# An attention and token-mixing kernel on one Trainium2 core: the second layer of the first group in float32, weight blocks merged in another order, and copies of the prologue moved ahead of exponentials

## The chip, the cores and the metric

The kernel runs on one core of one Trainium2 chip. The metric is the device time of one execution in microseconds (us), as the median of several runs. The engines are named as in the profile: PE (TensorE, its matmuls), PEld (its weight loads), DVE (VectorE), ACT (ScalarE), POOL (GpSimd) and SP (SyncE, which issues the DMAs).

## The reference

Attention with exponential features over 8 batches, 8 heads, 576 rows and 64 columns, followed by a mixing over rows and a two-layer network over the 512 channels:

```python
def phi(x):                                   # w_phi is 64 x 128
    proj = np.einsum('bhsd,df->bhsf', x, w_phi)
    proj = proj - np.max(np.abs(proj), axis=-1, keepdims=True)
    return np.concatenate([np.exp(proj), np.exp(-proj)], axis=-1)
q_p, k_p = phi(q), phi(k)
kv = np.einsum('bhsf,bhsd->bhfd', k_p, v)
num = np.einsum('bhsf,bhfd->bhsd', q_p, kv)
den = np.einsum('bhsf,bhf->bhs', q_p, k_p.sum(axis=2))[..., None] + 1e-06
x = (num / den).transpose(0, 2, 1, 3).reshape(8, 576, 512)
u = x + (x.transpose(0, 2, 1) @ U @ V).transpose(0, 2, 1)    # U 576 x 32, V 32 x 576
out = u + np.maximum(u @ w_ch1, 0.0) @ w_ch2                 # 512 x 2048, 2048 x 512
```

q, k, v and w_phi are float32. U, V, w_ch1 and w_ch2 are float64; the kernel reads them as pairs of 32-bit words and makes float32 of them on the chip.

## The kernel before, in words

**Rows and groups.** The 8 × 576 rows are split into 512 rows of each batch and 64 left over. One batch's 512 rows are a group of the two-layer network; the 64 left over of all eight batches are a ninth group. A group has 16 `hidden` steps (line 688: 128 of the 2048 hidden channels by 512 rows, PSUM tile `ph`) and 16 `add` steps (line 712: those 128 channels times their rows of w2 into four PSUM tiles `o` of 128 rows each). Steps are called chunks; the list `todo` holds them, hidden f ahead of add f − 1.

**Two numbers for one.** The large matmuls run in fp32r. To keep float32's precision each operand is parted: `hi` is the value rounded to fp32r by a copy of ACT, `lo` is what is left, a subtraction on DVE, and a product is made of three matmuls, hi·hi, hi·lo and lo·hi. So a hidden step has 12 matmuls (line 695), an add 12 (line 719). `relu` (line 703) makes h_hi from `ph` on ACT (line 706) and h_lo on DVE (line 707).

**Weight blocks.** w1 and w2 are 32 blocks of 128×512, w1 and w2 in turn. `load_block` (lines 222 and 226) has SP load one of 512 KB into one of four buffers, tag `wide`. `convert` (line 135) takes a float64 apart: on DVE an and (141), a shift with an and (147) and an or (150), on ACT a copy of the low half (144) and a pass with a bias (145). `join` (154, a custom DVE instruction) adds the parts, tile `w_r`; `end_block` makes `w_hi` on ACT (243) and `w_lo` on DVE (244). `conv` does one slot: begin the next block, then end the block before it. The blocks' tiles live in the tags `wh1_f`, `wh2_f` and `wl0` to `wl32`, `w_r` of block i in the place of `wl(i+1)`; some of these places hold early tiles of the prologue before (`home`, line 267). U and V go through the same `convert` and `join`, in `uv_parts` (171 to 207), a generator that does one piece at each `next(uv)`.

**Attention.** A `Pair` is two heads of one batch; there are four to a batch. Its steps are `transpose_both` (T), `copy_both` (ACT copies of T, line 373, DVE's parts of T and tail_T, line 331), `whole_q` and `whole_k` (projections; k features at lines 412 and 414, copies of q at 436), the exponentials (ACT, 421 to 423), `end_q` (DVE's subtraction, 442 and 444, and q's exponentials, after POOL's all-reduce at 437), `s_kv` and `s_out`. Batches from the third on use parted T and w_phi (`w_hl`, `tail_T`; line 451 is the projection of a parted tail). `Tokens` is the mixing over rows with U and V (`split`, `down`, `up`), `Mixer` the two-layer network of one group. `keep_busy` (768) gives PE matmuls to do in waits.

**The order.** The program has two parts. `early` (802) is written by hand: the attention of batch 0, and beside it U, V and the first weight blocks; then, from chunk to chunk of group 0, the attention of pairs 4 to 7 and the other blocks, 23 chunks (hidden 0 to 11 and add 0 to 10) in all. In it PE, ACT, DVE and POOL all keep the order in which the code issues. `chunk(n, blocks)` does n chunks and `blocks` slots of `conv` behind each; a hidden's `relu` is held back until the next chunk (`held`). `ordered` (928) goes to the end of the program; only PE keeps the written order there, and a scheduler places the instructions of the others, into free places of the first part too. `boundary` (905) is the change from one group to the next.

## Time and profile before

| | |
|---|---|
| median of 3 runs | 1221.85 us (1221.19 to 1223.09) |
| the profiled execution, its own time | 1222.26 us |
| its span | 1220.3 us |
| its mean granted clock of TensorE | 0.964 |
| PE busy | 1134.9 us (93%), 9292 instructions |
| DVE busy | 669.6 us (55%), 1371 instructions |
| ACT busy | 537.4 us (44%), 1134 instructions |
| POOL busy | 153.3 us (13%), 119 instructions |
| share of PE's work by line | hidden (695) 235.8 + 229.8 + 229.1 us, add (719) 230.8 + 225.0 + 224.6 us |
| chain that ended last | PE 80%, DVE 11%, ACT 5%, SP's queue 2% |

The span runs from the first to the last instruction of the profiled execution; its time has some 2 us more around it. Busy shares are means over stages of quite different kinds, so the profile has to be read by windows of time. A timeline row has the start, the length, the engine, the line, the operation, out<-in, the tile's size and the number of instructions merged into the row (x1, x2); the bracket is the idle time of the engine just before it and what ended that. A row of the waits is the waiter, the releaser, the total of the waits, their number and the longest one. A matmul of plain float32 leaves two records.

### The profile page before, as it was taken

How to read it: one execution, taken by the hardware profiler on the slowest of the kernel's cores; microseconds unless marked ns; L12 is line 12 of the kernel's file. 1: busy time of each engine (PE TensorE's matmuls, PEld its weight loads, DVE VectorE, ACT ScalarE, POOL GpSimd, SP SyncE). 2: the span in 40 equal slices, each digit the busy share in tenths (PEclk: the TensorE clock that was granted, in tenths of full speed). 3: DMA queues.
4: the chain of work that ended last, by engine and by line, in shares of the span. 5: the costliest groups of instructions: out<-in, count | busy, mean ns of one | idle time of the engine just before them, and what ended most of it. 6: DMA issues, size and time to landing. Idle time of an engine off the chain costs nothing.

```text
span 1220.3 us, 22461 instructions
## 1 busy us (share of the span) xinstructions
PE 1134.9 (93%) x9292; PEld 948.3 (78%) x9300; DVE 669.6 (55%) x1371; ACT 537.4 (44%) x1134; POOL 153.3 (13%) x119
## 2 busy tenths in 40 slices
PE   7756787599999999999999999999999999999997
PEld 5545565488888888888888888888888888888886
DVE  4776777766546655655565556655555644212111
ACT  7566666653445444544544454445443542111010
POOL 3310101110112011201111111111110210000000
PEclk9767988899999999999999999999999999999999
DMA  4344333212111311221113111211122002200001
GB/s 134 94 131 137 116 113 107 75 56 92 40 31 48 110 31 31 57 102 30 39 51 109 31 31 56 86 57 30 30 88 70 21 18 70 91 1 18 18 1 35
DMA packets 90533, 75.74 MB, mean 62 GB/s; under 512 B 51648, under 2 KB 76736, under 8 KB 90304
## 3 DMA queue, kind: packets, MB, share of 16 engines
q1 hardware_dynamic: 90432, 74.31, 20.1%
q8 instruction: 74, 1.21, 0.4%
q14 instruction: 27, 0.22, 0.1%
HBM read 55.41 MB, written 18.87 MB: 61 GB/s over the span
## 4 chain that ended last, share of the span: by engine, by line
PE 80%; DVE 11%; ACT 5%; SPq 2%; issue 1%; DMA 1%; ACTq 0%; DVEq 0%
PE ph L695 30%; PE o L719 29%; PE xp L564 5%; PE kv_ps L539 4%; PE pk L499 2%; PE T L389 2%; PE pp L650 1%; PE pt L682 1%; ACT w_hi L243 1%; DVE w_r L154 1%; DVE w_lo L244 1%; DVE w_r L150 1%; PE pq L520 1%; PE xp L557 1%; PE kv_ps L529 1%
## 5 line engine op out<-in xcount | busy, mean ns | idle before, releaser
L695 PE MATMUL ph<-uT_hi,w_hi 128*128 128x512 f32 x576 | 235.8, 409 | 36.8 <-DVE h_lo L707 33.9
L707 DVE SCALAR_TENSOR_TENSOR h_lo<-ph,h_hi 128x512 fp32r<-128x512 f32 x144 | 99.3, 690 | 282.6 <-ACT h_hi L706 282.6
L706 ACT ACTIVATE h_hi<-ph 128x512 fp32r<-128x512 f32 x144 | 85.8, 596 | 333.2 <-PE ph L695 332.5
L719 PE MATMUL o<-w_hi,h_hi 128*128 128x512 f32 x576 | 230.8, 401 | 0.0
L695 PE MATMUL ph<-uT_lo,w_hi 128*128 128x512 f32 x576 | 229.8, 399 | 0.7 <-DVE uT_lo L262 0.7
L695 PE MATMUL ph<-uT_hi,w_lo 128*128 128x512 f32 x576 | 229.1, 398 | 0.0
L719 PE MATMUL o<-w_hi,h_lo 128*128 128x512 f32 x576 | 225.0, 391 | 0.0
L719 PE MATMUL o<-w_lo,h_hi 128*128 128x512 f32 x576 | 224.6, 390 | 0.0
L695 PEld LDWEIGHTS ph<-uT_hi,w_hi 128*128 128x128 f32 x576 | 111.1, 193 | 63.4 <-DVE h_lo L707 37.2
L437 POOL PARTITION_ALL_REDUCE qp<-qp x64 | 128.1, 2013 | 213.0 <-ACT qp L436 212.4
L695 PEld LDWEIGHTS ph<-uT_hi,w_lo 128*128 128x128 f32 x576 | 110.9, 192 | 24.6
L695 PEld LDWEIGHTS ph<-uT_lo,w_hi 128*128 128x128 f32 x576 | 111.3, 193 | 22.1 <-DVE uT_lo L262 1.3
L719 PEld LDWEIGHTS o<-w_hi,h_lo 128*128 128x128 f32 x576 | 108.1, 188 | 23.4
L719 PEld LDWEIGHTS o<-w_hi,h_hi 128*128 128x128 f32 x576 | 108.3, 188 | 20.5
L719 PEld LDWEIGHTS o<-w_lo,h_hi 128*128 128x128 f32 x576 | 108.5, 188 | 19.9
L437 POOL PARTITION_ALL_REDUCE qp_t<-qp_t x32 | 24.3, 759 | 636.0 <-ACT qp_t L436 636.0
L331 DVE TENSOR_TENSOR T<-T,T 64x512 fp32r<-64x512 f32 x96 | 66.1, 689 | 23.7 <-ACT T L330 21.7
L330 ACT CAST T<-T 64x512 fp32r<-64x512 f32 x96 | 55.8, 581 | 29.2 <-DVE T L331 19.1
L564 PE MATMUL xp<-kv,qp 128*64 128x65 f32 x2048 | 68.5, 227 | 0.0
L564 PEld LDWEIGHTS xp<-kv,qp 128*64 128x64 f32 x2048 | 65.8, 144 | 0.0
L539 PE MATMUL kv_ps<-vb,kp 128*64 128x65 f32 x2048 | 65.4, 221 | 0.2 <-ACT kp L423 0.2
L539 PEld LDWEIGHTS kv_ps<-vb,kp 128*64 128x64 f32 x2048 | 64.3, 138 | 0.3 <-ACT kp L423 0.3
(132 smaller groups left out, 1443.8 us busy)
## 6 DMA issues: line engine op xcount, KB each, us to landing
w<-in_moe_w_ch_dram SPq DMA_DIRECT2D x32, 512.0 KB, 3.7
raw<-in_k_dram SPq DMA_DIRECT2D x32, 256.0 KB, 3.0
raw<-in_q_dram SPq DMA_DIRECT2D x32, 256.0 KB, 2.7
vb<-in_v_dram SPq DMA_DIRECT2D x64, 128.0 KB, 3.1
u_dram<-x SPq DMA_DIRECT2D x32, 256.0 KB, 2.6
st<-u_dram SPq DMA_DIRECT2D x16, 512.0 KB, 3.8
out_dram<-st SPq DMA_DIRECT2D x32, 256.0 KB, 2.8
t_r<-in_k_dram SPq DMA_DIRECT2D x32, 32.0 KB, 2.1
```

Source lines behind the costliest of these rows:

```text
L150: nc.vector.scalar_tensor_tensor(out=a, in0=hi_w, scalar=-0x80000000, in1=a, op0=ALU.bitwise_and, op1=ALU.bitwise_or)
L330: nc.scalar.copy(out=dst[0:D], in_=src)
L331: nc.vector.tensor_sub(dst[D:2 * D], src, f32(dst[0:D]))
L389: nc.tensor.transpose(out=pT[:, c * P:(c + 1) * P], in_=self.raw[n][:, c // 2, c % 2, :], identity=ident)
L437: nc.gpsimd.partition_all_reduce(qp[0], qp[1], P, ReduceOp.absmax)
L499: nc.tensor.matmul(pk[:, i, :, :], self.T[0][:, i, cs], w_hl, start=True, stop=True)
L539: nc.tensor.matmul(self.kv_v[z * HP:(z + 1) * HP, f, g, :], kp[f][:, i, z * HP:(z + 1) * HP], self.vb[:, g, t, :], start=False, stop=(t == ...
L564: nc.tensor.matmul(xv[zs, c, :], qp[f][:, c * P + z * HP:c * P + (z + 1) * HP], self.kv[:, f, c // 2, :], start=(f == 0), stop=(f == 1), s ...
L695: nc.tensor.matmul(ph, l[:, c * P:(c + 1) * P], r[:, c, :], start=(n == 0), stop=(n == len(terms) * NCC - 1))
L706: nc.scalar.activation(out=h_hi, in_=ph, func=AF.Relu)
L707: nc.vector.scalar_tensor_tensor(out=h_lo, in0=ph, scalar=0.0, in1=f32(h_hi), op0=ALU.max, op1=ALU.subtract)
L719: nc.tensor.matmul(self.o[t], l[:, cs], r, start=(f == 0 and n == 0), stop=(f == NFC - 1 and n == len(terms) - 1))
```

## The change

**The second layer of group 0.** `relu` of group 0 writes one float32 tile `h` on ACT and no h_lo. Its `add` multiplies `h` with the merged block `w_r` of w2 (kept in `w_t`) in one float32 matmul a tile in place of three fp32r ones: 4 matmuls a step in place of 12. The parting of w2 moves to `split_w2`, which `hidden` of group 1 calls, one block a step.

**The blocks.** `conv` now begins with ACT's copy of the new block's low half, then merges the block before it (`join`, and w_hi where it is of w1) through the argument `between` of `convert`, then issues the rest of the new block, and then `w_lo` of the block before, where it is of w1. The places of `w_r` change to suit. `chunk` issues its slots of `conv` between a hidden's matmuls and its `relu`; `held` is gone, and the number of slots per chunk is another.

**The prologue and the order.** `copy_both` and `whole_q` of the next pair come ahead of `end_q` of this one; pieces of U and V are converted behind `s_out`; in the last pairs of the first part `end_q` is later.

```diff
-    def convert(st, a, b_):
+    def convert(st, a, b_, between=None):
...
+        nc.scalar.activation(out=bh[:, :, 0], in_=halves[:, :, 1], func=AF.Copy, scale=2.0 ** -13)
+        if between is not None:
+            between()
         nc.vector.tensor_scalar(
             out=bh[:, :, 1], in0=halves[:, :, 3], scalar1=0x7FF0, scalar2=None,
             op0=ALU.bitwise_and)
-        nc.scalar.activation(out=bh[:, :, 0], in_=halves[:, :, 1], func=AF.Copy, scale=2.0 ** -13)
...
+    def merge_block():
+        f, m, b_, r = begun[ended[0]]
+        join(r.bitcast(I32), b_)
+        if m == 2:
+            w_t[f] = r
+            return
+        hi = const.tile([P, C], F32R, tag=f"wh1_{f}", name=f"w_hi1_{f}")
+        nc.scalar.copy(out=hi, in_=r)
+        w_hi_t[1, f] = hi
...
     def end_block():
+        f, m, b_, r = begun[ended[0]]
+        if m == 1:
+            lo = const.tile([P, C], F32R, tag=f"wl{f}", name=f"w_lo1_{f}")
+            nc.vector.tensor_sub(lo, r, f32(w_hi_t[1, f]))
+            w_lo_t[1, f] = lo
...
+    def split_w2(f):
+        r = w_t.pop(f)
+        hi = const.tile([P, C], F32R, tag=f"wh2_{f}", name=f"w_hi2_{f}")
+        lo = const.tile([P, C], F32R, tag=f"wl{NFC + f}", name=f"w_lo2_{f}")
         nc.scalar.copy(out=hi, in_=r)
         nc.vector.tensor_sub(lo, r, f32(hi))
...
     def conv(n=1):
...
+            some = ended[0] < len(begun)
             if len(begun) < NB:
-                begin_block()
-            if ended[0] < len(begun) - 1 or len(begun) == NB and ended[0] < NB:
+                i = len(begun)
+                f, m = i // 2, i % 2 + 1
+                at = NFC + (f + 1 if m == 2 else (f + 2) % (NFC + 1))
...
+                convert(loaded[i], r.bitcast(I32), b_, merge_block if some else None)
+                begun.append((f, m, b_, r))
+            elif some:
+                merge_block()
+            if some:
                 end_block()
...
         def hidden(self, f, later=False):
+            if self.g == 1:
+                split_w2(f)
...
         def relu(self, f, ph):
+            if self.g == 0:
+                h = moe.tile([P, 512], F32, tag="h_hi", bufs=2, name=f"h{self.g}_{f}")
+                nc.scalar.activation(out=h, in_=ph, func=AF.Relu)
+                self.h[f] = h
+                return
...
             terms = self.h[f]
+            if self.g == 0:
+                terms = ((terms, w_t[f]),)
...
     def chunk(n=1, blocks=0):
         for _ in range(n):
             fn, f, *ts = todo.pop(0)
...
+            if fn.__name__ == "hidden":
+                rest = fn(f, True)
+                conv(blocks)
                 rest()
...
             p[i + 1].transpose_both()
             keep_busy(2)
+            p[i + 1].copy_both()
+            p[i + 1].whole_q()
+            keep_busy(2)
             p[i].end_q()
-            p[i + 1].copy_both()
...
             if i == 1:
+                next(uv)
                 next(uv)
                 tk.split(0)
             if i == 2:
+                next(uv)
                 next(uv, None)
-                conv()
+                conv(2)
...
             p[i].whole_k()
+            if i > 5:
+                p[i - 1].end_q()
             chunk(2, 1)
...
+            chunk(2, 1)
             p[i].whole_q()
             chunk(1, 2)
             if i == 6:
                 tk.down(0)
-            p[i].end_q()
-            chunk(1, 1)
-            if i == 7:
-                p[8].transpose_k()
-            chunk(1, 1)
+            if i < 7:
+                chunk(1, 2)
+        p[8].transpose_k()
+        p[7].end_q()
+        chunk(1, 2)
```

Where the instructions stand follows from this and from the scheduler. The first place is a weight block on DVE in the middle of the first part. Before, with w_b and w_r of the block under way, w_r_5 and w_lo_5 of the one before it:

```order
L147 TENSOR_SCALAR w_r_6_1611<-w_6_1416 128x512
L150 SCALAR_TENSOR_TENSOR w_r_6_1611<-w_6_1416,w_r_6_1611 128x512
L154 ISA w_r_5_1566<-w_r_5_1566,w_b_5_1565 128x1024
L244 TENSOR_TENSOR w_lo_5_1619<-w_r_5_1566,w_hi_5_1618 128x512
L141 TENSOR_SCALAR w_b_6_1624<-w_6_1446 128x512
```

The same place on DVE in the changed kernel, with the two blocks numbered 6:

```order
L156 ISA w_r_6_1575<-w_r_6_1575,w_b_6_1574 128x1024
L144 TENSOR_SCALAR w_b_6_1584<-w_6_1514 128x512
L149 TENSOR_SCALAR w_r_6_1585<-w_6_1514 128x512
L152 SCALAR_TENSOR_TENSOR w_r_6_1585<-w_6_1514,w_r_6_1585 128x512
L246 TENSOR_TENSOR w_lo_6_1594<-w_r_6_1575,w_hi_6_1588 128x512
L156 ISA w_r_6_1585<-w_r_6_1585,w_b_6_1584 128x1024
L144 TENSOR_SCALAR w_b_7_1604<-w_7_1530 128x512
```

Between the join (ISA) and the w_lo of a block stand three instructions of the next block, where there was none, and a block of w2 has no w_lo here. The same blocks on ACT, before:

```order
L144 ACTIVATE w_b_6_1610<-w_6_1416 128x512
L145 ACTIVATE w_b_6_1610<-w_b_6_1610,warm 128x512
L243 CAST w_hi_5_1618<-w_r_5_1566 128x512
L144 ACTIVATE w_b_6_1624<-w_6_1446 128x512
L145 ACTIVATE w_b_6_1624<-w_b_6_1624,warm 128x512
L243 CAST w_hi_6_1632<-w_r_6_1611 128x512
```

And in the changed kernel, where h_4 is a float32 tile of group 0 and w_hi_6_3173 the first of the two parts of a w2 block:

```order
L141 ACTIVATE w_b_6_1584<-w_6_1514 128x512
L239 CAST w_hi_6_1588<-w_r_6_1575 128x512
L147 ACTIVATE w_b_6_1584<-w_b_6_1584,warm 128x512
L728 ACTIVATE h_4_1596<-ph_4_1559 128x512
L141 ACTIVATE w_b_7_1604<-w_7_1530 128x512
L255 CAST w_hi_6_3173<-w_r_6_1585 128x512
L147 ACTIVATE w_b_7_1604<-w_b_7_1604,warm 128x512
```

The copy w_hi stands between the two passes of the next block, where it stood behind both; the copies w_hi of w2 (line 255) are issued by group 1 and placed by the scheduler here, a block apart, in the first part.

The second place is DVE at the end of the first part, where tail_T of the first parted pair (line 331 before, 351 after) is made. Before:

```order
L154 ISA w_r_14_2427<-w_r_14_2427,w_b_14_2426 128x1024
L244 TENSOR_TENSOR w_lo_14_2469<-w_r_14_2427,w_hi_14_2468 128x512
L331 TENSOR_TENSOR T_2_0_2480<-T_2_0_2475,T_2_0_2480 64x512 x2
L331 TENSOR_TENSOR tail_T_0_2474<-tT_0_2472,tail_T_0_2474 64x2x64 x2
L707 SCALAR_TENSOR_TENSOR h_lo_11_2502<-ph_11_2447,h_hi_11_2501 128x512
L141 TENSOR_SCALAR w_b_15_2505<-w_15_2412 128x512
L147 TENSOR_SCALAR w_r_15_2506<-w_15_2412 128x512
```

After:

```order
L246 TENSOR_TENSOR w_lo_15_2314<-w_r_15_2297,w_hi_15_2308 128x512
L256 TENSOR_TENSOR w_lo_0_2723<-w_r_0_883,w_hi_0_2722 128x512
L351 TENSOR_TENSOR T_2_0_2326<-T_2_0_2321,T_2_0_2326 64x512
L256 TENSOR_TENSOR w_lo_1_2783<-w_r_1_1112,w_hi_1_2782 128x512
L256 TENSOR_TENSOR w_lo_2_2836<-w_r_2_1195,w_hi_2_2835 128x512
L351 TENSOR_TENSOR T_2_0_2326<-T_2_0_2321,T_2_0_2326 64x512
L351 TENSOR_TENSOR tail_T_0_2320<-tT_0_2318,tail_T_0_2320 64x2x64
L256 TENSOR_TENSOR w_lo_3_2969<-w_r_3_1327,w_hi_3_2968 128x512
L351 TENSOR_TENSOR tail_T_0_2320<-tT_0_2318,tail_T_0_2320 64x2x64
L464 TENSOR_TENSOR qp_3_t<-qp_3_t 128x128
L464 TENSOR_TENSOR qp_3_0_2274<-qp_3_0_2274 128x512
L464 TENSOR_TENSOR qp_3_1_2277<-qp_3_1_2277 128x512
```

Four subtractions of w2's parting (line 256) stand among those of T and tail_T, the q subtractions (line 464) of the last early pair come behind them, and the last block's work, which followed tail_T, is ahead of it.

The third place is ACT in the prologue, at the second pair's q features. Before:

```order
L423 ACTIVATE qp_1_t<-qp_1_t 128x128
L422 ACTIVATE qp_1_00_333<-qp_1_01_334 128x512
L423 ACTIVATE qp_1_01_334<-qp_1_01_334 128x512
L422 ACTIVATE qp_1_10_337<-qp_1_11_338 128x512
L423 ACTIVATE qp_1_11_338<-qp_1_11_338 128x512
L373 COPY T_0_2_436<-T_0_2_438 128x512
L376 COPY tail_T_2_434<-tT_2_448 64x2x64 x2
L379 COPY T_0_2_435<-T_0_2_443 128x512
L144 ACTIVATE u_st<-u_st 128x160
L145 ACTIVATE u_st<-u_st,warm 128x160
L436 COPY qp_2_01_538<-pq_0_2_531 128x512
```

After:

```order
L393 COPY T_0_2_437<-T_0_2_439 128x512
L396 COPY tail_T_2_435<-tT_2_449 64x2x64 x2
L399 COPY T_0_2_436<-T_0_2_444 128x512
L456 COPY qp_2_01_465<-pq_0_2_458 128x512
L456 COPY qp_2_11_469<-pq_0_2_459 128x512
L456 COPY qp_2_t<-pqt_2_462 128x128
L442 ACTIVATE qp_1_t<-qp_1_t 128x128
L443 ACTIVATE qp_1_t<-qp_1_t 128x128
L442 ACTIVATE qp_1_00_278<-qp_1_01_279 128x512
L443 ACTIVATE qp_1_01_279<-qp_1_01_279 128x512
```

The three T copies and three q copies of the third pair now stand ahead of the six q exponentials of the second, and the conversion of U is no longer between them.

More of the change, by code (lines that the diff above doesn't have):

```diff
@@ L207, in uv_parts @@
             nc.vector.tensor_sub(vm[lo], v_f[lo], f32(vm[lo]))
-    w_hi_t, w_lo_t = {}, {}
+    w_hi_t, w_lo_t, w_t = {}, {}, {}
     NB = 2 * NFC
@@ L227, in load_block @@
         loaded.append(st)
-    def begin_block():
-        i = len(begun)
-        f, m = i // 2, i % 2 + 1
-        b_ = const.tile([P, C], I32, tag=f"wh{m}_{f}", name=f"w_b{m}_{f}")
-        r = const.tile([P, C], F32, tag=f"wl{i + 1}", name=f"w_r{m}_{f}")
-        convert(loaded[i], r.bitcast(I32), b_)
-        begun.append((f, m, b_, r))
-    def end_block():
-        i = ended[0]
-        f, m, b_, r = begun[i]
-        join(r.bitcast(I32), b_)
-        hi = const.tile([P, C], F32R, tag=f"wh{m}_{f}", name=f"w_hi{m}_{f}")
-        lo = const.tile([P, C], F32R, tag=f"wl{i}", name=f"w_lo{m}_{f}")
+    def merge_block():
[7 more added lines that the diff above has]
+        w_hi_t[1, f] = hi
+    def end_block():
+        f, m, b_, r = begun[ended[0]]
[3 more added lines that the diff above has]
+            w_lo_t[1, f] = lo
+        begun[ended[0]] = None
+        ended[0] += 1
+    def split_w2(f):
+        r = w_t.pop(f)
+        hi = const.tile([P, C], F32R, tag=f"wh2_{f}", name=f"w_hi2_{f}")
+        lo = const.tile([P, C], F32R, tag=f"wl{NFC + f}", name=f"w_lo2_{f}")
         nc.scalar.copy(out=hi, in_=r)
         nc.vector.tensor_sub(lo, r, f32(hi))
-        w_hi_t[m, f], w_lo_t[m, f] = hi, lo
-        begun[i] = None
-        ended[0] += 1
+        w_hi_t[2, f], w_lo_t[2, f] = hi, lo
     def conv(n=1):
@@ L253, in conv @@
                 load_block()
+            some = ended[0] < len(begun)
             if len(begun) < NB:
-                begin_block()
-            if ended[0] < len(begun) - 1 or len(begun) == NB and ended[0] < NB:
+                i = len(begun)
+                f, m = i // 2, i % 2 + 1
+                at = NFC + (f + 1 if m == 2 else (f + 2) % (NFC + 1))
+                b_ = const.tile([P, C], I32, tag=f"wh{m}_{f}", name=f"w_b{m}_{f}")
+                r = const.tile([P, C], F32, tag=f"wl{at}", name=f"w_r{m}_{f}")
+                convert(loaded[i], r.bitcast(I32), b_, merge_block if some else None)
[3 more added lines that the diff above has]
+            if some:
                 end_block()
@@ L268, in tile_kernel @@
     homes = [f"wh{m}_{f}" for f in range(NFC - 1, KEEP - 1, -1) for m in (1, 2)]
-    homes += [f"wl{i}" for i in range(2 * NFC, 2 * KEEP, -1)]
+    homes += [f"wl{f}" for f in range(NFC - 1, KEEP - 1, -1)]
+    homes += [f"wl{NFC + i}" for i in (*range(NFC, KEEP + 1, -1), 0)]
     home_of = {("xs1", t): homes[t] for t in range(NT + 1)}
@@ L782, in tile_kernel @@
     ORDERED = 7
-    held = []
     def chunk(n=1, blocks=0):
@@ L789, in chunk @@
             fn, f, *ts = todo.pop(0)
-            rest = held.pop() if held else None
-            if rest is not None and fn.__name__ == "hidden":
+            if fn.__name__ == "hidden":
+                rest = fn(f, True)
+                conv(blocks)
                 rest()
-                rest = None
-            if fn.__name__ == "hidden":
-                held.append(fn(f, True))
             else:
                 fn(f, *ts)
-                if rest is not None:
-                    rest()
-            conv(blocks)
+                conv(blocks)
     def early(x, xt):
@@ L822, in early @@
             keep_busy(2)
+            p[i + 1].copy_both()
+            p[i + 1].whole_q()
+            keep_busy(2)
             p[i].end_q()
-            p[i + 1].copy_both()
-            if i == 1:
-                next(uv)
             p[i].s_kv()
             p[i + 2].load_v()
-            keep_busy(2)
-            if i == 2:
-                next(uv)
-            p[i + 1].whole_q()
             p[i + 1].whole_k()
+            keep_busy(1)
             if i == 2:
@@ L861, in early @@
         m = Mixer(0, x)
-        m.transposes(0)
-        m.transposes(1)
-        conv()
-        tk.up(NT)
-        m.transposes(2)
-        m.transposes(3)
-        p[4].end_q()
-        conv(2)
+        for t in range(NT):
+            m.transposes(t)
+        conv(1)
         todo.extend(m.chunks())
@@ L872, in early @@
         p[4].s_kv()
+        tk.up(NT)
+        p[4].end_q()
         chunk(1, 1)
@@ L893, in early @@
                 tk.down(0)
-            p[i].end_q()
-            chunk(1, 1)
-            if i == 7:
-                p[8].transpose_k()
-            chunk(1, 1)
+            if i < 7:
[3 more added lines that the diff above has]
+        chunk(1, 2)
         while ended[0] < NB:
             conv()
-        while held:
-            held.pop()()
         return p[7], p[8], x, xt, tk
```

10 lines of the change are left out of this document (5 added, 5 removed).

## Prediction

> **What bounds the kernel now.** I read the page's slices first, for where TensorE is not full. The rows are the busy tenths of each engine in 40 slices of 30.5 us, and the clock that TensorE was granted.
>
> ```profile
> PE   7756787599999999999999999999999999999997
> DVE  4776777766546655655565556655555644212111
> PEclk9767988899999999999999999999999999999999
> ```
>
> From the ninth slice on PE is full and its clock is high; ahead of that nothing is full. Then I split the span where that changes. The first hidden chunk starts near 94 us and the weights begin to be converted near 62 us. The end of the first stage is the instruction on which PE waits for the last time at length:
>
> ```profile
> 244.65 0.48 PE L451 MATMUL pkt<-w_hl,tail_T 128*128 128x128 f32 x1 [10.93 <-DVE tail_T L331]
> ```
>
> I call this time T*: 244.65 us. The windows around it (window, length, then busy time and count of PE, weight loads, DVE, ACT, POOL, then the granted clock, the DMA engines' share and GB/s):
>
> ```profile
> 0.00:62.00 62.00, 46.67 (x652) 35.51 (x661) 37.69 (x101) 38.34 (x86) 21.45 (x32) 0.89 0.43 119
> 62.00:244.65 182.65, 124.62 (x1053) 97.82 (x1048) 136.66 (x271) 116.57 (x207) 20.83 (x15) 0.82 0.36 112
> 244.65:330.00 85.35, 83.92 (x685) 70.97 (x687) 54.44 (x108) 40.42 (x88) 9.20 (x6) 0.97 0.21 63
> 530.00:1220.30 690.30, 680.44 (x5131) 573.97 (x5128) 324.80 (x650) 248.28 (x543) 69.44 (x45) 1.00 0.15 46
> ```
>
> Behind T* PE is busy 98 to 99% of the time, so what comes there can only get longer by PE's own work. Between 62 and T* PE is busy 68%, DVE 75%, ACT 64%: three engines wait for each other. The chain of waits there, in rows of waiter, releaser, total us, times, longest:
>
> ```profile
> PE ph L695 <- DVE h_lo L707: 28.6, 6, 9.1
> DVE w_lo L244 <- ACT w_hi L243: 26.7, 30, 1.8
> ACT w_hi L243 <- DVE w_r L154: 23.5, 23, 2.1
> ACT w_b L145 <- DVE w_b L141: 16.9, 24, 2.9
> DVE h_lo L707 <- ACT h_hi L706: 12.0, 7, 4.1
> PE pkt L451 <- DVE tail_T L331: 10.9, 1, 10.9
> SPq L226 <- DVE w_r L150: 63.8, 14, 10.5
> SPq L222 <- DVE w_r L150: 41.0, 13, 8.1
> ```
>
> PE waits for DVE, DVE waits for ACT, ACT for DVE again: a ping-pong inside every weight block. One block on DVE, of 30 alike in this stage:
>
> ```profile
> 154.26 0.45 DVE L141 TENSOR_SCALAR w_b<-w 128x512 uint16<-128x512 uint16 x1
> 154.61 0.41 DVE L147 TENSOR_SCALAR w_r<-w 128x512 int32<-128x512 int32 x1
> 155.05 0.69 DVE L150 SCALAR_TENSOR_TENSOR w_r<-w,w_r 128x512 int32<-128x512 int32 x1
> 155.66 0.69 DVE L154 CUSTOM_DVE_ANT_0 w_r<-w_r,w_b 128x1024 uint16<-128x1024 uint16 x1
> 157.08 0.69 DVE L244 TENSOR_TENSOR w_lo<-w_r,w_hi 128x512 fp32r<-128x512 f32 x1 [0.74 <-ACT w_hi L243]
> 157.69 0.45 DVE L141 TENSOR_SCALAR w_b<-w 128x512 uint16<-128x512 uint16 x1
> ```
>
> Start to start the five cost 0.35, 0.44, 0.61, 0.68 (1.42 less the wait) and 0.61 us, 2.69 in all. The wait stands because w_hi reads what the join wrote one instruction earlier, and w_lo reads w_hi.
>
> **The change: the stage from 62 us to T\*.** I take DVE as the pacemaker, the busiest of the three and the releaser in PE's longest waits.
>
> *Work that goes from DVE.* Fifteen of the w_lo of w2 leave (15 × 0.61 = 9.2 us), and eleven h_lo of group 0 (same size and form; 0.61 each is an estimate from the w_lo row, 6.7 us). What comes in ahead of T*: block 15's second half starts earlier, and one join and one w_lo of it are now in front (0.35+0.44+0.61+0.68+0.61 = 2.7). The scheduler does not keep the parting of w2 in group 1: four of the new subtractions stand ahead of the last tail_T (4 × 0.61 = 2.4), and ACT's sixteen copies w_hi of w2 stand right behind the joins, where they stood. So ACT is relieved of nothing. Three q subtractions move behind T* (two of 128x512, one of 128x128: about 1.4). Net −9.2 −6.7 +2.7 +2.4 −1.4 = −12.2 us: DVE's work falls from 136.7 to 124.5.
>
> *Waits that go.* DVE idles 182.65 − 136.66 = 46.0 us. Of it 26.7 is w_lo behind w_hi and 12.0 h_lo behind h_hi, 38.7 together; 7.3 has other causes and stays. The join now has the next block's copy, and the and, shift and or, between it and w_lo, and group 0 has no h_lo.
>
> *Waits that come.* The join now runs first in a slot and needs ACT's bias pass of the block before; w_lo stands behind ACT's exponentials where a slot meets them; ACT's w_hi waits for a join that stands behind k features on DVE. Behind a waiting w_lo or join stand, on DVE, the next block's three instructions and now and then the k features and T subtractions, for which PE waits. ACT work in front costs, from its start times here, 0.63, 0.72 and 0.49 us an instruction:
>
> ```profile
> 98.59 0.76 ACT L144 ACTIVATE w_b<-w 128x512 uint16<-128x512 uint16 x1
> 99.22 0.85 ACT L145 ACTIVATE w_b<-w_b,warm 128x512 uint16<-128x512 uint16 x1
> 99.94 0.59 ACT L243 CAST w_hi<-w_r 128x512 fp32r<-128x512 f32 x1
> ```
>
> I went along the new order with these prices and found some 14 us of waits of 1 to 2.7 us, and add 5 for those I can't see: 19. This is the softest term: 5 at least (one short wait in each of three pairs), at most the 38.7 that went. I take the middle because ACT has 116.6 us of work in a stage of about 150, and can't be early everywhere. Stage: 124.5 + 7.3 + 19 = 150.8 us in place of 182.65.
>
> A cross-check by pairs, from one T copy of ACT to the next:
>
> ```profile
> 114.33:156.96 42.63, 32.22 (x272) 25.38 (x271) 31.24 (x61) 27.63 (x48) 5.18 (x4) 0.92 0.40 123
> 156.96:202.30 45.34, 33.82 (x264) 26.54 (x264) 34.27 (x67) 29.37 (x54) 5.36 (x4) 0.81 0.31 100
> 202.30:244.65 42.35, 29.27 (x263) 22.73 (x261) 31.67 (x63) 27.01 (x49) 4.93 (x3) 0.89 0.31 92
> ```
>
> No engine has over 34.3 us of work in a pair. Walked by hand with the new order and the prices above, these take about 31, 36 and 34.5 us, and the 52.3 us ahead of them 40.5: 142 together. The walk knows only undisturbed instructions, and some are stretched:
>
> ```profile
> 182.24 1.43 DVE L141 TENSOR_SCALAR w_b<-w 128x512 uint16<-128x512 uint16 x1
> ```
>
> That one took 1.43 in place of 0.45. I allow 5.5 us for such over the stage (an estimate, some six of them), 147.5 in all, 3 us from the sum by idle time.
>
> *Ahead of 62 us.* The T and q copies of the next pair now stand ahead of this pair's q exponentials on ACT, and the converting of U and V behind the second and third s_out. Two waits of DVE, the brackets below, are what that is placed on:
>
> ```profile
> 30.21 0.33 DVE L154 CUSTOM_DVE_ANT_0 u_st<-u_st 128x320 uint16<-128x320 uint16 x1 [3.38 <-ACT u_st L145]
> 51.29 0.42 DVE L154 CUSTOM_DVE_ANT_0 v_st<-v_st 128x512 uint16<-128x512 uint16 x1 [3.05 <-ACT v_st L145]
> ```
>
> They are 6.4 us; I take 5.5 (2, if the exponentials that now come later are missed by PE; 8, with the earlier T copies on top). T* falls to 62 − 5.5 + 150.8 = 207.3, that is −37.3 us.
>
> **The change: PE's own work.** Group 0's second layer goes from three f32r matmuls a tile to one in float32. The f32r price, and float32 elsewhere:
>
> ```profile
> 1140.10 0.39 PE L695 MATMUL ph<-uT_hi,w_hi 128*128 128x512 f32 x1
> 1140.32 0.39 PE L695 MATMUL ph<-uT_lo,w_hi 128*128 128x512 f32 x1
> 292.15 2.72 PE o L719 x12
> L480 PE MATMUL pq<-T,w_f x32: 589/664/1217, 6.4 to 222.6; 64*128 64x512 f32 x32
> 17.14 1.13 PE L480 MATMUL pq<-T,w_f 64*128 64x512 f32 x4 [1.41 <-ACT T L373]
> 117.44 0.38 PE L458 MATMUL pkt<-w_f,tail_T 128*128 128x128 f32 x2
> 117.75 1.16 PE L463 MATMUL pk<-w_f,T 64*128 64x128 f32 x16
> ```
>
> An f32r matmul starts every 0.2275 us (2.73 for an add of twelve, 2.72 in the chain) and its record is 0.39 long, so 0.16 of a record is not throughput. The shortest float32 record of the same width is 0.589: less 0.16 that is 0.43, about two passes, and a float32 matmul leaves two records (x2 for one pkt). So 2 × 0.43 = 0.85 to 4 × 0.2275 = 0.91; four make an add of 3.41 to 3.64, and I take 3.55, +0.8. The low end is the four records of pq in 1.13 us as two matmuls one after another, 0.57 each, an add of 2.3 (but these have 64 rows each, and pk's sixteen records in 1.16 us say that such ones run side by side). The high end is the pkt's 0.31 for 128 columns times four: 1.24, an add of 4.96.
>
> The Trainium skill, page FP8 and Floating Point Precision, section TensorE Precision Notes, speaks against the change: float32 takes four passes through the array, one more than the three terms here. An estimate by that rule is 4/3 of 2.73, 3.64, an add dearer by 0.91, where the records give 0.8; no run so far shows the new matmul itself.
>
> Eleven of the sixteen adds come ahead of T*, in PE's 58 us of idle time; five come behind and are paid: +4.0 (−2.1 to +11.2). Behind T* the boundary also gets the moved q subtractions and twelve more w_lo of w2 on DVE. PE is 98% busy there and DVE 64% (54.4 of 85.4 us), so I put +1.0 on it (0 to 2.5). Group 1 on is otherwise the same work under a full PE.
>
> **The sum.** The profiled execution took 1222.26 us for a span of 1220.3, 2.0 us around it, and is 0.4 above the median of the runs shown. 1222.26 − 37.3 + 4.0 + 1.0 = 1190.0 us.
>
> **The rivals.**
>
> *Weak gain.* New waits of DVE on ACT take the place of the old ones in proportion: DVE stays 75% busy, and 124.5 us of work take 124.5/0.748 = 166.4. T* is then 222.9, the time 1205.5. For it: ACT keeps all its work, and the subtractions of w2 land just ahead of T*. Against: the 26.7 us have one cause, a distance of one instruction, and that distance grows. Chance 0.16.
>
> *Dear float32.* An add costs 4.96: five behind T* cost +11.2, and eleven ahead of it 24.5 us more PE work, of which perhaps 5 lands on T* beside the waits. 1222.26 − 37.3 + 5 + 11.2 + 1 = 1202. For it: pkt's spacing. Against: the 0.589 record. Chance 0.08.
>
> *Strong gain.* New waits are only the 5 us: the stage is 136.8, T* 193.3, the time 1176. PE's work up to there (124.6 us now, at a clock of 0.82) would have to fit with the eleven dearer adds. Chance 0.12.
>
> *Slower: the weight blocks' loads set the pace.*
>
> ```profile
> w<-in_moe_w_ch_dram SPq DMA_DIRECT2D x32, 512.0 KB, 3.7
> ```
>
> If one block in four buffers can't be had faster than 182.65/32 = 5.7 us, the stage keeps its length, and only the dearer adds and the boundary are paid: 1222.26 + 5 = 1227. For it: SP stands 104.8 us in these loads. Against: what SP waits for is DVE's w_r that frees the buffer, a load lands in 3.7 us with others under way, and no engine's wait on a load is among the rows above. Chance 0.04.
>
> *The change doesn't do what it says.* In part that is seen already: w_hi of w2 stays early. Were the stage all ACT's, nothing would come of it, 1222. Chance 0.02.
>
> **How the numbers follow.** Forecast 0.58: 1190. The rivals are 0.16 (1205.5), 0.08 (1202), 0.12 (1176), 0.04 (1227), 0.02 (1222). The range takes in the weak gain and the dear float32 up to 1207, and reaches down to 1177, which the forecast gives with new waits of 6 us; what is left out is the strong gain beyond that and the two cases at 1222 and above. About 0.2%, 2.4 us, is what a measurement of this kernel can tell from no change. Faster 0.94, same 0.02, slower 0.04.
>
> **What would show it.** In the profile after: w_lo's waits on w_hi fall from 26.7 to under 10 us and no h_lo of group 0 is there; the last tail_T releases PE near 207 us; an add of group 0 takes 3.4 to 3.7 us in the chain; behind T* PE stays full, with some 980 us to the end. It is wrong if T* stays above 223, if DVE is still idle for over 35 us ahead of it, or if an add takes over 4.5 us.

## The result, and the profile after

The changed kernel takes 1183.72 us (median of 4 runs, 1182.8 to 1187.0); the kernel before, run beside it, 1221.98 us. The ratio is 0.969, with an interval of 0.967 to 0.971: 38 us less, where 32 were forecast. The profiled execution took 1184.01 us, its span is 1182.1 us.

The page's slices of the changed kernel (29.6 us each now):

```profile
PE   8759988999999999999999999999999999999997
DVE  4788898666565556555565656655665535112111
PEclk9869998999999999999999999999999999999999
```

TensorE still has its thin place in the third slice, but from the fourth on it is at 80% or more and the clock stays high; VectorE is at 80% or more from the third slice to the seventh, where before it was at 60 to 80%. The end of the first stage, T*:

```profile
203.69 0.47 PE L471 MATMUL pkt<-w_hl,tail_T 128*128 128x128 f32 x1 [5.39 <-DVE tail_T L351]
```

T* went from 244.65 to 203.7 us, 41 us earlier, and PE's wait for tail_T there is half as long. The windows (columns as before), the first from 62 us to T*, the second from there, and then the first one cut where the first hidden chunk begins:

```profile
62.00:203.70 141.70, 121.79 (x979) 83.41 (x980) 121.32 (x246) 109.06 (x202) 21.36 (x15) 0.91 0.46 143
203.70:330.00 126.30, 125.03 (x1051) 99.78 (x1052) 77.34 (x159) 57.44 (x129) 16.50 (x11) 0.98 0.18 53
62.00:88.15 26.15, 16.70 (x127) 12.88 (x128) 21.10 (x47) 18.94 (x40) 5.20 (x4) 0.63 0.47 153
88.15:203.70 115.55, 105.10 (x852) 70.53 (x852) 100.22 (x200) 90.12 (x163) 16.16 (x11) 0.97 0.46 141
```

VectorE's work in the stage fell from 136.66 to 121.32 us, its idle time from 46.0 to 20.4 (141.70 − 121.32). Of the 41 us, 15 are less work and 26 are less waiting. From the first hidden on, PE is busy 105.1 of 115.6 us. The waits of the stage:

```profile
ACT w_hi L255 <- DVE w_r L156: 10.9, 9, 2.8
DVE w_r L156 <- ACT w_b L147: 7.6, 4, 2.6
PE pkt L478 <- issue: 11.6, 3, 7.6
PE pkt L471 <- DVE tail_T L351: 5.4, 1, 5.4
DVE w_lo L246 <- ACT w_hi L239: 5.4, 4, 2.0
ACT w_hi L239 <- DVE w_r L156: 4.1, 6, 1.2
```

PE's 28.6 us behind h_lo are gone with h_lo itself; w_lo waits for w_hi 4 times and not 30 times. New are the joins that wait for ACT's bias pass (w_r behind w_b, 7.6 us) and TensorE's 7.6 us ahead of a pkt. How the ping-pong went is to be seen in two weight blocks on DVE:

```profile
117.75 0.69 DVE L156 CUSTOM_DVE_ANT_0 w_r<-w_r,w_b 128x1024 uint16<-128x1024 uint16 x1
118.36 0.46 DVE L144 TENSOR_SCALAR w_b<-w 128x512 uint16<-128x512 uint16 x1
...
119.76 0.68 DVE L246 TENSOR_TENSOR w_lo<-w_r,w_hi 128x512 fp32r<-128x512 f32 x1
120.36 0.69 DVE L156 CUSTOM_DVE_ANT_0 w_r<-w_r,w_b 128x1024 uint16<-128x1024 uint16 x1
...
124.56 1.64 DVE L156 CUSTOM_DVE_ANT_0 w_r<-w_r,w_b 128x1024 uint16<-128x1024 uint16 x1 [2.10 <-ACT w_b L147]
```

The join at 117.75 and its w_lo at 119.76 have three instructions between them, and the w_lo has no bracket. The join at 124.56 shows the new wait: ACT does q copies (an attention step) ahead of the bias pass. This join is also stretched, 1.64 us in place of 0.69; what such rows have in common stands in the last section.

```profile
121.89 1.08 ACT L456 COPY qp<-pq 128x512 f32<-128x512 f32 x2 [0.18 <-PE pq L500]
122.85 0.28 ACT L456 COPY qp_t<-pqt 128x128 f32<-128x128 f32 x1
123.01 0.81 ACT L141 ACTIVATE w_b<-w 128x512 uint16<-128x512 uint16 x1
123.66 0.87 ACT L147 ACTIVATE w_b<-w_b,warm 128x512 uint16<-128x512 uint16 x1
```

An add of group 0 in the chain, two of those behind T*, and the record of its float32 matmuls (two to a matmul):

```profile
210.12 3.44 PE o L748 x8
222.04 3.43 PE o L748 x8
L748 PE MATMUL o<-w_r,h x40: 590/592/595, 210.0 to 245.8; 128*128 128x512 f32 x40
```

It takes 3.44 us, with a record every 0.43 us (each is 0.59 long), beside 2.73 before.

### The profile page after: what moved, and what is told of

Its sections match the earlier page's. It is cut to its first block, busy times and chain, and to the rows that moved or that the text cites. A ratio compares the mean times of both kernels' runs of the same rounds, so it can differ in the third digit from the quotient of the medians.

```text
span 1182.1 us, 22322 instructions
## 1 busy us (share of the span) xinstructions
PE 1134.0 (96%) x9231; PEld 928.6 (79%) x9236; DVE 655.9 (55%) x1355; ACT 531.9 (45%) x1134; POOL 153.5 (13%) x119
## 4 chain that ended last, share of the span: by engine, by line
PE 86%; DVE 8%; ACT 3%; issue 2%; DMA 1%; POOL 0%; SPq 0%; DVEq 0%; POOLq 0%; ACTq 0%
PE ph L717 31%; PE o L748 31%; PE kv_ps L559 5%; PE xp L584 4%; PE pk L519 2%; PE pp L670 2%; PE T L409 2%; PE pt L702 1%; PE kv_ps L549 1%; DVE w_r L156 1%; PE pq L540 1%; PE pq L541 1%; PE xp L577 1%; DVE w_r L152 1%; PE vp L686 1%
## 5 line engine op out<-in xcount | busy, mean ns | idle before, releaser
L734 DVE SCALAR_TENSOR_TENSOR h_lo<-ph,h_hi 128x512 fp32r<-128x512 f32 x128 | 88.3, 690 | 265.3 <-ACT h_hi L733 265.3
L717 PE MATMUL ph<-uT_lo,w_hi 128*128 128x512 f32 x576 | 225.9, 392 | 0.2 <-DVE uT_lo L281 0.2
L717 PE MATMUL ph<-uT_hi,w_lo 128*128 128x512 f32 x576 | 225.5, 391 | 0.0
L733 ACT ACTIVATE h_hi<-ph 128x512 fp32r<-128x512 f32 x128 | 76.3, 596 | 326.8 <-PE ph L717 326.3
L748 PE MATMUL o<-w_hi,h_hi 128*128 128x512 f32 x512 | 204.7, 400 | 0.0
L748 PE MATMUL o<-w_hi,h_lo 128*128 128x512 f32 x512 | 199.9, 390 | 0.0
L748 PE MATMUL o<-w_lo,h_hi 128*128 128x512 f32 x512 | 199.6, 390 | 0.0
L748 PEld LDWEIGHTS o<-w_hi,h_lo 128*128 128x128 f32 x512 | 96.1, 188 | 20.9
L748 PEld LDWEIGHTS o<-w_hi,h_hi 128*128 128x128 f32 x512 | 96.3, 188 | 18.2
L748 PEld LDWEIGHTS o<-w_lo,h_hi 128*128 128x128 f32 x512 | 96.4, 188 | 17.8
L350 ACT CAST T<-T 64x512 fp32r<-64x512 f32 x96 | 55.8, 581 | 29.6 <-DVE T L351 19.5
```

Source lines behind the costliest of these rows:

```text
L350: nc.scalar.copy(out=dst[0:D], in_=src)
L717: nc.tensor.matmul(ph, l[:, c * P:(c + 1) * P], r[:, c, :], start=(n == 0), stop=(n == len(terms) * NCC - 1))
L733: nc.scalar.activation(out=h_hi, in_=ph, func=AF.Relu)
L734: nc.vector.scalar_tensor_tensor(out=h_lo, in0=ph, scalar=0.0, in1=f32(h_hi), op0=ALU.max, op1=ALU.subtract)
L748: nc.tensor.matmul(self.o[t], l[:, cs], r, start=(f == 0 and n == 0), stop=(f == NFC - 1 and n == len(terms) - 1))
```

## The experiments

Times are medians; ratios are to the kernel before, run beside each on the same chip. Theory one says that VectorE, with its waits on ScalarE, sets the first stage; theory two has another cause in each run. T* is read in each as above.

### One edit taken back: the second layer in f32r

```diff
-        if m == 2:
-            w_t[f] = r
-            return
+        # w_hi and w_lo of both matrices in merge_block and end_block
-            if self.g == 0:
-                terms = ((terms, w_t[f]),)
```

h_lo of group 0 and the places of the tiles also go back to what they were before.

> The changed kernel, but group 0's second layer stays in three f32r matmuls a tile, with h_lo, and w2 is parted as its blocks are merged; block order and prologue are those of the change. Theory one (VectorE and its waits on ScalarE set the first stage): VectorE gets back fifteen w_lo of w2 and eleven h_lo at 0.61 us, 16 us, and up to 9 us of waits behind h_hi, so the stage ends 16 to 25 us later than at 203.7, at 220 to 229 us; five adds behind it are 0.7 us cheaper each. Time 1196 to 1205 us. Theory two (with the float32 layer or not, TensorE sets the stage once the blocks are in the new order): eleven adds are 0.7 us cheaper each, the stage ends at 204 or earlier, time 1176 to 1181.

Measured: 1189.9 us, ratio 0.974 (0.9725 to 0.9754). T* is 213.2, 9.5 us later than in the changed kernel, and the rest of the program 3 us shorter (975.4 in place of 978.4). Neither number fits: float32 is worth 6 us here, not 12 to 21, and not less than nothing. The window to T* and the waits:

```profile
62.00:213.20 151.20, 118.86 (x1024) 93.52 (x1024) 135.55 (x269) 110.11 (x202) 22.89 (x15) 0.88 0.44 136
```

```profile
DVE w_lo L242 <- ACT w_hi L236: 7.1, 5, 2.0
DVE h_lo L722 <- ACT h_hi L721: 2.1, 4, 0.5
```

VectorE has nearly the work of before, 135.6 us, in 151.2 us: it is 90% busy. So the rest of the change takes most of the waits out without float32, those behind h_hi too (the run with neither edit, below, shows that these don't need the order inside a block either). What float32 takes away on top is 14.2 us of work, of which a third comes back as idle time (15.7 us here, 20.4 with float32).

### Float32 alone

```diff
 (before.py)
+            if self.g == 0:
+                terms = ((terms, w_t[f]),)
+        if m == 2:
+            w_t[f] = r
+            return
```

The edit also moves the parting of w2 to group 1 and places the tiles as the change does; blocks, chunks and prologue are those of before.

> The kernel before with the float32 second layer of group 0 and the later parting of w2 alone; block order, chunks and prologue as before. Theory one: VectorE loses 16 us of work, 12 us of waits behind h_hi and the waits behind w_hi of the sixteen w2 blocks (half of 26.7, 13 us), less new waits; the stage ends 20 to 35 us ahead of 244.65 and the time is 1190 to 1206 us. Theory two (the block order is what frees the stage): the pairs of w_hi and w_lo of w1 still stand next to each other and the gain is under 12 us, 1211 us or more.

Measured: 1197.55 us, ratio 0.980 (0.9785 to 0.9814), inside theory one's range. T* is 217.5.

```profile
62.00:217.50 155.50, 123.53 (x1000) 84.33 (x996) 122.81 (x245) 112.79 (x206) 22.03 (x15) 0.89 0.43 131
```

```profile
DVE w_lo L249 <- ACT w_hi L248: 15.8, 15, 2.1
```

Work fell by 13.9 us and idle time by 13.3 (46.0 to 32.7). The w_lo of w1 still waits, 15 times for 1.05 us.

### A block's pieces in the old order

```diff
-        nc.scalar.activation(out=bh[:, :, 0], ...)
-        if between is not None:
-            between()
         nc.vector.tensor_scalar(out=bh[:, :, 1], ...)
+        nc.scalar.activation(out=bh[:, :, 0], ...)
...
         nc.vector.scalar_tensor_tensor(out=a, ...)
+        if between is not None:
+            between()
```

> The changed kernel, but a block's pieces on VectorE and ScalarE stand as before: and, copy, bias, shift, or, then join, w_hi and w_lo of the block before it next to each other. Theory one: sixteen w_lo of w1 wait again for the w_hi right ahead, 0.9 us each as before (26.7/30), 14 us, of which what stands ahead of the stage's end is paid; time 1192 to 1198 us. Theory two (TensorE sets the stage, 96 to 99% busy between 88 and 160 us): most of it is hidden, 1183 to 1187 us.

Measured: 1192.68 us, ratio 0.977 (0.9751 to 0.9787), as theory one has it. T* is 210.2.

```profile
62.00:210.20 148.20, 120.66 (x979) 81.88 (x979) 121.94 (x245) 110.23 (x202) 21.99 (x15) 0.94 0.44 136
```

```profile
DVE w_lo L246 <- ACT w_hi L239: 20.3, 16, 3.6
```

The work is the same, only waits come: 14.9 us more behind w_hi, and 6.4 less behind the bias pass (1.2 in place of 7.6).

### Neither of the two

The first and the third edit together.

> Neither the float32 second layer nor the new order inside a block: group 0 in f32r with w2 parted at once, join, w_hi and w_lo next to each other as before; what is left of the change is the prologue, the slots per chunk, the relu behind the slots and the later end_q. Theory one (float32 and the order inside a block remove the same waits, so that each alone does most of it): without both the waits of w_lo and h_lo come back and the stage ends at 225 to 240 us, time 1203 to 1217. Theory two (the slots and the place of relu and end_q do it, the other two add 6 and 9 us each on top): 1184 + 6 + 9, 1197 to 1201.

Measured: 1213.43 us, ratio 0.993 (0.9916 to 0.9947), T* 233.6: theory one.

```profile
62.00:233.59 171.59, 124.14 (x1022) 97.41 (x1023) 135.60 (x268) 113.03 (x201) 20.81 (x15) 0.86 0.38 117
```

```profile
DVE w_lo L242 <- ACT w_hi L236: 29.8, 31, 2.7
PE ph L710 <- DVE h_lo L722: 12.6, 5, 6.5
```

With this run the four corners are known, all of them with the rest of the change in place. The times are in us, and the columns on VectorE are for the window from 62 us to T*:

| | median | T* | VectorE's work | its idle time | w_lo behind w_hi | join behind bias pass |
|---|---|---|---|---|---|---|
| neither | 1213.4 | 233.6 | 135.6 | 36.0 | 29.8 | none |
| float32 alone | 1192.7 | 210.2 | 121.9 | 26.3 | 20.3 | 1.2 |
| the block's order alone | 1189.9 | 213.2 | 135.6 | 15.7 | 7.1 | none |
| both | 1183.7 | 203.7 | 121.3 | 20.4 | 5.4 | 7.6 |

Each alone gives 21 and 24 us, the second to come only 6 or 9. The work that float32 takes away is the same in both rows, 14 us; what doesn't add up is the idle time. It falls by 9.7 us with float32 and by 20.3 with the order, but only by 15.6 with both. Some 8 us of the difference are waits of w_lo that either edit removes, and 6 are the joins behind the bias pass, a wait that is long only where both edits are in.

All else in the change (prologue, slots, relu and end_q) gives the 9 us from 1222.4 to 1213.4. With neither edit no w_lo or h_lo of group 0 is saved, and still VectorE doesn't wait for h_hi ahead of T*, where before it waited 11.7 us (12.0 with one behind T*). So this wait went with the rest of the change; which part of it did that was not tried.

### One cost put back: h_lo

A run of the changed kernel in which VectorE makes h_lo of group 0, read by nothing:

```diff
                 self.h[f] = h
+                nc.vector.scalar_tensor_tensor(out=h_lo, in0=ph, scalar=0.0, in1=h, ...)
```

> The changed kernel with one thing put back: VectorE makes an h_lo for group 0 that nothing reads, a 128x512 subtraction behind each h. Theory one (VectorE sets the stage): 11 times 0.61 us, 6.7 us, and some 4 to 8 us of waits for h, so 1190 to 1199 us. Theory two (TensorE sets it): at most 3 us, 1184 to 1187 us.

Measured: 1192.78 us, ratio 0.977 (0.9751 to 0.978): theory one.

```profile
62.00:211.00 149.00, 123.09 (x980) 82.35 (x980) 128.71 (x257) 108.92 (x201) 21.81 (x15) 0.92 0.44 135
PE pkt L471 <- DVE tail_T L351: 8.6, 1, 8.6
```

VectorE's work rose by 7.4 us and T* by 7.3, and its idle time stayed (20.3 us, with new waits of h_lo for h in place of others): the work is passed on, as far as one profile of each kernel can tell, for the first hidden starts 1 us earlier here than in the changed kernel. TensorE, though over 90% busy behind the first hidden in the changed kernel, gave no cover, because what is late is at the end of VectorE's queue: the wait for tail_T grows from 5.4 to 8.6.

### The prologue as before

```diff
-            p[i + 1].copy_both()
-            p[i + 1].whole_q()
             p[i].end_q()
+            p[i + 1].copy_both()
...
             if i == 2:
-                next(uv)
                 next(uv, None)
                 conv(2)
```

> The changed kernel, but with the loop over the first three pairs in the order of before (copies and q of the next pair behind this pair's q exponentials, U and V converted where they were), with two block slots at its end as in the change. Theory one (the prologue pays in full): the two waits of VectorE on ScalarE, 6.4 us, come back and the first hidden starts about 5.5 us later than 88.15, time 1188 to 1191 us. Theory two (its gain is made good by the fuller chunks behind it, or eaten by the 7.6 us for which TensorE stands at 57.9 us in the changed kernel): within 2 us, 1182 to 1186.

Measured: 1185.61 us, ratio 0.970 (0.9691 to 0.9717), which can't be told from the changed kernel's: theory two. The first hidden starts at 88.96 us, 0.8 later than with the new prologue. PE's waits in this run and in the changed kernel:

```profile
66.68 0.77 PE L478 MATMUL pkt<-w_f,tail_T 128*128 128x128 f32 x2 [5.14 <-issue]
```

```profile
65.55 0.77 PE L478 MATMUL pkt<-w_f,tail_T 128*128 128x128 f32 x2 [7.61 <-issue]
```

What the new order wins earlier, it waits 2.5 us longer for here. The 0.8 us are less than what the starts of single executions differ by (last section).

### The first blocks behind the copies

```diff
             if i == 2:
-                next(uv)
-                next(uv, None)
-                conv(2)
...
         p[4].whole_k()
+        next(uv)
+        next(uv, None)
+        conv(2)
         p[3].s_out(x, xt)
```

> The changed kernel, with the last pieces of V and the first two block slots moved behind the fifth pair's T copies and k features. In the changed kernel ScalarE does these pieces first and the T copies at 64.5 us, though their matmuls are done at 55; TensorE stands 7.6 us. Theory one (that queue on ScalarE is a new wait that the change brought): TensorE's gap of 7.6 us goes, the stage behind begins 4 to 6 us earlier, time 1178 to 1180 us. Theory two (VectorE's work sets the stage, and it was busy through that gap): the blocks are only done later by as much, time 1182 to 1186.

Measured: 1185.58 us, ratio 0.970 (0.9688 to 0.9715): theory two. The gap ahead of pkt went, and came back further down:

```profile
75.78 2.75 PE L670 MATMUL pp<-xs,u_all 128*128 128x256 f32 x10 [13.95 <-ACT xs L656]
```

It was 3.2 us in that place; 13.95 is more than 7.6 and 3.2 together. The first hidden starts at 88.73 us. This fits theory two: what VectorE and ScalarE have to do ahead of the first hidden decides, not where in it TensorE waits.

### w2 parted later

```diff
-        hi = const.tile([P, C], F32R, tag=f"wh2_{f}", ...)
-        lo = const.tile([P, C], F32R, tag=f"wl{NFC + f}", ...)
+        hi = const.tile([P, C], F32R, tag=f"wl{NFC + f}", ...)
+        lo = const.tile([P, C], F32R, tag=f"wh2_{f}", ...)
```

> The changed kernel, but w_hi and w_lo of w2 change places in memory, so that w_hi can't be written before group 0's add of the block before is done; eleven or so of the sixteen copies then stand behind the first stage on ScalarE, and one VectorE subtraction fewer ahead of its end. Theory one (ScalarE's copies, with 10.9 us of waits for the joins, hold up what VectorE waits for): the stage ends 3 to 6 us earlier, time 1178 to 1181. Theory two (VectorE's own work sets it): less than 2 us, 1182 to 1185.

Measured: 1183.83 us, ratio 0.969 (0.967 to 0.9702): no difference, theory two. In the profile 3 of the copies stand ahead of T* and not 15. The copies w_hi that the scheduler hoists into the first stage cost nothing that can be measured.

### The transposes at the end of the stage earlier

```diff
             p[i].whole_q()
+            if i == 7:
+                p[8].transpose_k()
             chunk(1, 2)
...
-        p[8].transpose_k()
         p[7].end_q()
```

> The changed kernel, with the transposes of the ninth pair's k one chunk earlier, so that VectorE makes its T and tail_T ahead of the last two blocks. In the changed kernel TensorE waits 5.4 us for tail_T at 198.3 us, and VectorE does four w_lo of w2 (2.9 us) just ahead of it. Theory one (the end of the stage is that wait): 4 to 5.5 us less, time 1178 to 1180. Theory two (the last blocks are then late for the next hidden, and TensorE waits for them): within 1.5 us, 1182 to 1185.

Measured: 1180.01 us, ratio 0.966 (0.9644 to 0.9678). The median is 3.7 us below the changed kernel's, though the intervals overlap by a hair. The wait for tail_T is gone, T* is 197.2; TensorE in the stretch from the first hidden:

```profile
86.97:197.20 110.23, 105.28 (x851) 70.36 (x852) 93.81 (x191) 87.58 (x159) 15.31 (x11) 0.98 0.48 147
```

Now TensorE is busy 105.3 of 110.2 us and VectorE 93.8: with the tail out of the way TensorE is the busiest. Of T*'s 6.5 us, 1.2 are there at the first hidden already (86.97 and 88.15 us), up to which the two kernels are alike. Another part is given back behind T*, where a hidden waits 2.2 us for an h that it didn't wait for.

### Both, and one slot later

> The changed kernel with the ninth pair's transposes one chunk earlier and w_hi of w2 parted later, both at once. Theory one (TensorE is the bound of the stage from 88 us on: 105.3 of 110.2 us busy with the transposes earlier): nothing on top of the transposes, 1179 to 1181.5 us. Theory two (ScalarE's early copies still cost something): 1176 to 1178.5 us.

The last two edits at once: 1181.61 us, ratio 0.9675 (0.9661 to 0.9689). Nothing on top, as theory one has it, though the median is 0.1 us above its range.

```diff
 (with the transposes earlier)
             if i == 2:
...
-                conv(2)
+                conv(1)
```

> The changed kernel with the transposes earlier and one block slot fewer ahead of the first hidden chunk (one in place of two behind the third s_out; the last slot moves to the end). Theory one (VectorE's and ScalarE's work ahead of the first hidden sets when TensorE's full stretch begins, as the moved but not shorter gap of the run with blocks behind the copies says): one slot is 2.7 us of VectorE and 2.2 us of ScalarE, so the first hidden starts 2 to 3 us earlier and the time is 1177 to 1178.5 us. Theory two (the slot is then missing behind it, and a hidden waits for its block): 1180 us or more.

Measured: 1178.64 us (1178.51 to 1179.77), ratio 0.9646 (0.9633 to 0.9659), just outside the forecast and the best of all; its interval lies clear below that of the change. The first hidden starts at 82.2 us:

```profile
62.00:82.19 20.19, 16.36 (x127) 12.45 (x128) 16.66 (x39) 15.82 (x34) 4.18 (x3) 0.66 0.32 103
82.19:192.89 110.70, 105.11 (x851) 70.05 (x852) 91.99 (x188) 86.66 (x157) 16.53 (x13) 0.98 0.53 161
PE ph L717 <- ACT h L728: 3.8, 1, 3.8
```

T* is 4.3 us earlier than with the transposes alone, more than the one slot's 2.7, but only 1.4 us of the median remain: 3.8 us are waited for behind it. Both theories hold a part.

### f32r with the transposes earlier

> Group 0 in f32r, with w2 parted at once, in the order of the change (as in the first experiment, 1189.9 us), and with the ninth pair's transposes one chunk earlier. Theory one (with that much work on VectorE, it still sets the stage, 113.9 of 124.7 us busy): the wait of 7.5 us for tail_T goes in part, 1184 to 1187 us, and float32 stays 4 to 7 us ahead. Theory two (once the end doesn't wait for VectorE, TensorE's cheaper adds count, 0.7 us sixteen times): 1175 to 1180 us, as fast as float32 or faster.

Measured: 1191.76 us, ratio 0.9755 (0.9741 to 0.9768): slower than either theory has it, and no gain over the 1189.9 of the first experiment. The profiled execution, 1194.41 us, is the longest of its four. The stretch from the first hidden to T*, and TensorE's waits for h_lo behind T*:

```profile
90.72:212.12 121.40, 104.09 (x896) 82.59 (x897) 108.58 (x214) 88.64 (x159) 16.05 (x11) 0.94 0.44 134
```

```profile
PE ph L710 <- DVE h_lo L722: 6.3, 2, 5.1
```

The wait of 7.5 us for tail_T went, and one of 5.1 us for h_lo came 6 us behind T* (the other, 1.2 us, is in the changed kernel too). VectorE's queue is as long as before, and whoever is served first, another waits. With float32 the same edit gains 3.7 us; VectorE was busy 85% of the stretch from the first hidden there, and 89% here. That this room makes the difference is an argument from these figures and not shown by itself.

## Why the prediction was right, step by step

**The pacemaker and its work: right.** VectorE's work in the stage was put at 124.5 us and was 121.3; h_lo put back, 7.4 us of work that nothing reads, moved T* by 7.3 us. The four subtractions of w2 ahead of tail_T are there, and the copies w_hi of w2 stayed early, without harm (1183.8 us with most of them later).

**The waits that go and come: right in sum, 6 us too dear.** w_lo behind w_hi was to fall under 10 us and is 5.4; idle time was put at 7.3 + 19 = 26.3 and is 20.4. The 19 us were the softest term. Where one was looked for it stands (a join behind a late bias pass, up to 2.6 us, four times), but the w_lo that waits for an exponential in front of its w_hi is rare. What the working missed is where the waits belong. It counted 12.0 us behind h_hi as saved by leaving out h_lo; these are gone with h_lo in place too (none with neither edit, 2.1 us with the order alone). And the 26.7 us behind w_hi are taken by either edit in part: 9.5 us fewer with float32 alone, 22.7 with the order alone, 24.4 with both (from the 29.8 with neither).

**Ahead of 62 us, −5.5: the step that failed.** VectorE's first instruction on a weight block, in the kernel before, in the changed kernel and with the prologue as before:

```profile
62.96 0.45 DVE L141 TENSOR_SCALAR w_b<-w 128x512 uint16<-128x512 uint16 x1
```

```profile
60.85 0.46 DVE L144 TENSOR_SCALAR w_b<-w 128x512 uint16<-128x512 uint16 x1
```

```profile
61.98 0.46 DVE L144 TENSOR_SCALAR w_b<-w 128x512 uint16<-128x512 uint16 x1
```

So 2.1 us are won ahead of the stage and not 5.5, 1.1 of them by the order of the prologue. These are rough, for in the other runs with the new prologue and the blocks in their place this instruction stands between 59.9 and 63.2 us. The time moves by 1.9 us with the order of the prologue, inside the intervals. The two waits of 6.4 us on ACT are gone, but others took their place. VectorE's idle time ahead of 62 us is 25.2 us, where it was 24.3, and it waits 11.3 us for kv_ps (0.8 before). One reason is that TensorE now has the next pair's q projection ahead of kv_ps, and this projection waits for a T copy of ACT:

```profile
DVE kv L566 <- PE kv_ps L559: 11.3, 3, 4.4
41.29 2.08 PE L500 MATMUL pq<-T,w_f 64*128 64x512 f32 x4 [6.79 <-ACT T L393]
```

The first hidden did come 5.7 us earlier (93.88 to 88.15), but 3.6 of these are won behind the first weight block, where the blocks and the fifth pair's steps stand in another order. Before, a block's slot stood between the second and the third uT_hi on ACT (from 89.31 to 92.76 us), and the first hidden waited 2.95 us for uT_hi; in the changed kernel the four uT_hi follow one another, and it waits 0.67. No run takes this step back alone, so how much of the 3.6 us it is stays open.

**T\*: near, in part by luck.** T* was put at 207.3 us and came at 203.7. Counted from the first weight block, the prologue gave 3.4 us less than forecast, and the stage behind it took 7.0 us less than forecast (142.9 us; 1 of the 7 is work, 6 are waits). The two errors have opposite signs.

**The price of a float32 add: right.** 3.55 was forecast, 3.44 measured, +0.71 an add. The rule of the Trainium skill, page FP8 and Floating Point Precision, section TensorE Precision Notes, four passes, makes 3.64; the measured matmul is 0.86 us, 3.8 f32r matmuls, so it agrees within 6%. Five adds behind T* are +3.5; from T* to the end there are 978.4 us in place of 975.65, +2.8, so the boundary costs −0.8 and not +1.0.

**The rivals.** The weak gain fell: VectorE is 86% busy in the stage, not 75%. Dear float32 fell by the 3.44. The loads as the pacemaker fell too: with 28% more GB/s (143 in place of 112) no engine waits on a block's load for long enough to be in the list of waits. The strong gain (1176) is not reached by the change, but nearly by the version with the transposes and one slot later, 1178.6. What seems to bar the way further stands in the prediction only as an aside to that rival: with the tail out of the way TensorE is busy 105 of 110 us. One rival was not put forward: the granted clock of TensorE in the stage rose from 0.82 to 0.91, and a faster TensorE could have had a part in the gain. It doesn't set T* here: with the blocks in the old order the clock was 0.94 and with h_lo put back 0.92, and T* was 6.5 and 7.3 us later all the same.

## What to carry to other kernels

When two engines hand a tile back and forth, first put other work between the two handovers; that cost no instruction and was worth 24 us here, and cutting work gave 21 us alone but only 6 on top. Two edits that touch the same waits need not add, because each may take what the other would have taken and the two together may bring a new wait: measure each without the other before adding up their terms. Before an idle gap in a prologue is counted as a gain, look at what else must be done before the next long stretch, and by whom; here a 7.6 us gap that was taken away came back within a wait of 13.95 us a few steps later.
